# K's minus half on ScalarE by heads, q's softmaxes listed sooner, and three smaller moves in a two-branch linear attention

## The chip, the cores and the metric

The kernel runs on one core of one Trainium2 chip. The metric is the device time of one execution in microseconds (us); lower is better. The core has five engines that run side by side: TensorE (matrix products), VectorE (DVE in the profile), ScalarE (ACT), GpSimd (POOL) and SyncE (SP, which here only issues DMAs). Each has its own queue of instructions and works through it in order.

## The reference

Two branches A and B do the same on the same `x` with their own weights, and a gate mixes them. For one branch, with 2048 rows, 448 columns and 16 heads of 28:

```python
qkv = (x @ wqkv).reshape(B, S, 3, H, Dh).transpose(2, 0, 3, 1, 4)
pq = einsum("bhsd,hdf->bhsf", q, w_phi);  pk = einsum("bhsd,hdf->bhsf", k, w_phi)
phi_q = concatenate([softmax(pq), softmax(-pq)], -1)
phi_k = concatenate([softmax(pk), softmax(-pk)], -1)
kv = einsum("bhsf,bhsd->bhfd", phi_k, v);  z = phi_k.sum(over s)
num = einsum("bhqf,bhfd->bhqd", phi_q, kv)
den = einsum("bhqf,bhf->bhq", phi_q, z) + 1e-6
branch = (num / den) @ wo
...
g = sigmoid((x * gate_w).sum(-1))
out = g * branch_A + (1 - g) * branch_B
```

Everything is float32. So each row has, in each of 32 heads (16 of A, 16 of B), a plus half `softmax(p)` and a minus half `softmax(-p)`, for K and for Q.

## The kernel before, in words

The 2048 rows are 16 tiles of 128. `x` comes transposed, in eight pairs of tiles. TensorE multiplies in a rounded float32 form; to keep precision every operand is split into a high part and a low part (`split_x`, `split_wv`), and a product is 11 matmuls (`XT`: high by high, high by low, low by high).

**Start.** V's weights arrive in two halves (b = 0 is A with the gate's column, b = 1 is B), are split, and `v_first` (L394) computes V of tiles 0 and 1 together, a half at a time. Tile 0 goes to PSUM banks VA and VB, tile 1 borrows the two banks of K (`v_bank`, L387). `load_wp` (L305) brings the feature weights `phi` by four DMAs from ScalarE's queue. `fold` (L321) multiplies them into K's and then Q's projection, so that K and Q come out of TensorE as `p`; it needs `phi` and the loaded weights.

**K phase.** For each tile: `k_proj` (22 matmuls) into one PSUM pair of banks K, copied to `pk` by ScalarE (L439). `k_soft` (L429) then does the two softmaxes over the 28 features of each head: DVE takes the maximum and the minimum (L440, L441); GpSimd subtracts, `pk - max` and `min - pk` (L442, L443); ScalarE takes the exponential of each half in place (L446); DVE sums the heads (L447) and inverts (L448); GpSimd scales (L449). `pk`, `mx` and `sm` have two buffers, the result `e` three. `kv_acc` multiplies the result with V, two tiles at a time. Between them stand V of later tiles, and `q_proj` and `q_front` of Q, which subtract the maximum and send the tile through DRAM (`qd`) to bring four rows' heads together.

**Q's softmaxes** (`q_soft`, "S" in the list): a load from `qd`, exponential, minimum, subtraction, exponential, two sums, a scale, and a DVE transpose (L502) into one of four slots `eT`. One buffer `eq` serves all tiles, so the next tile begins behind that transpose. Tiles 0 to 7 are written to DRAM (`spill`) and fetched later; tiles 8 and 9 stay in slots 0 and 1; tiles 10 to 15 (`JIT = 10`) are done in the last phase.

**Last phase.** After K's last tile: `num` (L530) multiplies two tiles of Q's features with the turned `kv`, DVE transposes the result (L548), `mix` (L553) divides and applies the gate on GpSimd, `o_turn` transposes and splits, `out_mm` does 21 matmuls for each output tile, 42 for a pair.

**Gates.** `gates` (L510) inverts the logits on DVE, sends them through DRAM with five SP DMAs, and ends with a GpSimd operation (L518) that computes 1 - g. It is called for tiles 0 to 11 and, in the last phase, for 12 to 15.

**Order.** `steps()` lists the work; each function records its instructions with `Plan.add`: engine, estimated cost, keys read and written. `Plan.order` (L53) keeps TensorE's instructions in the listed order and lets the others go by a due time, worked backwards from what depends on them. The keys serve only this planning; the waits on the chip follow from the tiles that the instructions truly touch.

Of the kernel before, what the change touches and what calls it, by code (L numbers as in the profile page):

```python
# [9 lines left out]
AF = mybir.ActivationFunctionType  # L10
# [97 lines left out]

def steps():

    yield from (("V01", 0), ("V01", 1), ("FK", 0), ("x1",), ("V", 2), ("FK", 1), ("wq", 0), ("wq", 1), ("V", 3), ("x", 2))
    yield from (("FQ", 0), ("V", 4, 0), ("FQ", 1), ("later",), ("K", 0), ("V", 4, 1), ("K", 1), ("wo_rows",))
    yield from (("Q", 0), ("S", 0, 0), ("K", 2), ("Q", 1), ("S", 1, 1), ("kv", 0, 1), ("K", 3), ("V", 5))
    for p in range(2, 8):
        if p < 7:
            yield "x", p + 1
        yield "K", 2 * p
        yield "Q", 2 * p - 2
        if 2 * p - 2 < JIT:
            yield "S", 2 * p - 2, 0  # L120
        yield "kv", 2 * p - 2, 2 * p - 1
        yield "wo", p - 2
        if p in (3,):
            yield "wo", 6
        if p < 6:
            yield "V", 2 * p + 2
        yield "K", 2 * p + 1
        if p < 7:
            yield "Q", 2 * p - 1
            if 2 * p - 1 < JIT:  # L130
                yield "S", 2 * p - 1, 1
        if p < 6:
            yield "V", 2 * p + 3
        if p == 6:
            yield "gates", 0, 12
# [24 lines left out]
SPILL = list(range(JIT - 2))  # L160


# [1 line left out]
def hedgehog_mix(ctx: ExitStack, tc: tile.TileContext, xd, wv, wkt, wqt, wphi, wo, cmask, cpmask, out):  # L164
# [140 lines left out]
    def load_wp():  # L305
        add("DVE", 0.15, lambda: V.memset(wp, 0.0), [], [("wp", q) for q in range(4)])
        for q in range(4):
            add("ACT", 0.45, lambda q=q: A.dma_start(wp[32 * q:32 * q + DH], wphi[DH * q:DH * q + DH]), [], [("wp", q)], lat=3)
# [66 lines left out]
    def xkeys(t):  # L375
        return [("x", t // 2 % NX, t % 2), ("xl", t // 2 % NX, t % 2)]
# [14 lines left out]
        o, n = ((0, D + 2), (VB, D))[b]  # L391
        return [x[:, :, o:o + n] for x in (wvh, wvl)], n

    def v_first(b):  # L394

        w, n = v_weights(b)
        parts = [([(c, i, c)], [("x", 0, t) for t in range(2)] + [("v" + "hl"[i], c, b)])
                 for c, i in ((0, 0), (1, 0), (0, 1), (2, 0), (1, 1), (3, 0), (2, 1), (3, 1))]
        parts.append(([(4 + c, 0, c) for c in range(3)], xkeys(0) + xkeys(1)))
        for terms, keys in parts:  # L400
            def go(terms=terms):
                for xc, l, c in terms:
                    for t in range(2):
                        n_, k = v_bank(t, b)
                        nc.tensor.matmul(bank[n_][:, k, :n], xs[0][:, xc, t * P:t * P + P], w[l][:, c], start=(xc, l) == (0, 0), stop=xc == 6)
            add("PE", 2 * len(terms) * 0.203, go, keys, [v_bank(t, b)[0] for t in range(2)])
        for t in range(2):
            v_out(t, b)

    def v_proj(t, b):  # L410
# [13 lines left out]

    def k_proj(t, b):
        add("PE", 11 * 0.197, mms(t, feat((wkh, wkl), b), "K", b, FO, FZ),
            xkeys(t) + [("k", h, j, b) for h in "hl" for j in range(4)], ["K"])

    def k_soft(t):  # L429
        def p4():  # L430
            return fm(bank["K"][:, :, FO:FO + D])
        pk, kp = pks[t % 2].rearrange("p b (h f) -> p b h f", f=DH), ("pk", t % 2)
        mx, sm, e, n = mxs[t % 2], sms[t % 2], es[t % NE], t % NE
        ke, km = [("e", n, s) for s in range(2)], [("mx", t % 2, s) for s in range(2)]
        pkh = pk.rearrange("p b h f -> p (b h) f")
# [5 lines left out]
        put("DVE", 2 * D, lambda: V.tensor_reduce(mh[1], pkh, AX.X, OP.min), [kp], [km[1]])  # L441
        put("POOL", 2 * D, tt("POOL", e4[0], pkh, bc[0], OP.subtract), [kp, km[0]], [ke[0]])  # L442
        put("POOL", 2 * D, tt("POOL", e4[1], bc[1], pkh, OP.subtract), [kp, km[1]], [ke[1]])  # L443
        for s in range(2):
            e3 = e[:, s].rearrange("p (h f) -> p h f", f=DH)
            put("ACT", 2 * D, act(e[:, s], e[:, s], AF.Exp), [], [ke[s]])  # L446
            put("DVE", 2 * D, lambda s=s, e3=e3: V.tensor_reduce(sm[:, s], e3, AX.X, OP.add), [ke[s]], [("sm", t % 2, s)])  # L447
# [36 lines left out]
    def q_soft(k, slot):  # L484
# [10 lines left out]
        for s in range(2):  # L495
            e3 = eq[:, s].rearrange("p a c f -> p (a c) f")[:, :, :DH]
            put("DVE", 2 * D, lambda s=s, e3=e3: V.tensor_reduce(qsm[:, s], e3, AX.X, OP.add), [ke[s]], [("qsm", s)])  # L497
# [4 lines left out]
        add("DVE", 2.25, lambda: V.transpose(eTf[slot], eq.rearrange("p s a c f -> p (s a c f)")), ke, [("eT", slot)])  # L502

    def spill(k, slot):
        add("SP", 0.4, dma(ed[k], eTf[slot]), [("eT", slot)], [("ed", k)], lat=3, kb=1048)
# [4 lines left out]
    def gates(lo, hi):  # L510
        gl = glog[:, lo:hi]
        kl = [("gl", t) for t in range(lo, hi)]
        add("DVE", 0.1, lambda: V.tensor_scalar(gl, gl, 1.0, None, op0=OP.add), [], kl)
        add("DVE", 0.2, lambda: V.reciprocal(gl, gl), [], kl)
        add("SP", 0.4, dma(gd[:, lo:hi], gl), kl, [("gd", lo)], lat=2)
        for r in range(4):
            add("SP", 0.4, dma(gate[32 * r:32 * r + 32, 0, :, lo:hi], gd[:, lo:hi].rearrange("(c t) n -> t c n", c=4)), [("gd", lo)], [("ga", lo, r)], lat=2)
        add("POOL", 0.25, lambda: G.tensor_scalar(gate[:, 1, :, lo:hi], gate[:, 0, :, lo:hi], -1.0, 1.0, op0=OP.mult, op1=OP.add),  # L518
            [("ga", lo, r) for r in range(4)], [("gate", t) for t in range(lo, hi)])

    def kv_turn():
        for b in range(2):
# [79 lines left out]
    for b in range(2):  # L602
        for c in range(4):
            load_wv(c, b)
        if b == 0:
            load_wp()
    split_x(0, 0, P, "DVE")
    split_x(0, P, 2 * P, "DVE", "DVE")
    for b in range(2):
        for c in range(4):  # L610
            split_wv(c, b, "DVE" if b == 0 else "POOL")
    load_x(1)
    for b in range(2):
        load_wt(wkt, b)
# [27 lines left out]
    for what, *a in steps():  # L642
# [1 line left out]
            for b in a[1:] or (0, 1):  # L644
                v_proj(a[0], b)
        elif what == "V01":
            v_first(a[0])
        elif what == "K":
            if a[0] == 0:
                plan.hand_over([("x1raw",), *[("wvr", c, b) for c in range(4) for b in range(2)]], [("e", n, s) for n in range(NE) for s in range(2)])  # L650
# [42 lines left out]
            fetch(*a)  # L693
        elif what == "gates":
            gates(*a)
        else:
            {"later": later, "wo_rows": wo_rows, "load_wo": load_wo, "free_k": lambda: plan.hand_over(["K", "VA", "VB"], ["N"], free_k),
             "free_q": lambda: plan.hand_over(["Q"], ["O1", "T1"], free_q), "kv_turn": kv_turn,
# [50 lines left out]
```

## Time and profile before

| what | value |
|---|---|
| median of 3 runs | 352.05 us (349.84 to 352.11) |
| the profiled execution's own time | 351.24 us |
| its span in the profile | 349.5 us |
| granted TensorE clock | 1.00 |
| DVE busy | 277.7 us (79%) |
| ScalarE busy | 143.5 us (41%) |
| GpSimd busy | 245.0 us (70%) |

The profile is that of one execution. The span goes from its first instruction to its last; 1.74 us of the time lie outside it. A busy time is the sum over one engine's instructions with overlaps counted once. "Idle before, releaser" behind a row tells how long the engine had stood still and what ended that. "issue" as a releaser is time in which the engine waited for nothing that the profile shows.

### The profile page before, as it was taken

What the parts mean: (1) busy time and instruction counts of PE and PEld (TensorE: products, weight loads), DVE (VectorE), ACT (ScalarE), POOL (GpSimd) and SP (SyncE); (2) the same over time, 40 slices, a digit from 0 to 9 for tenths busy, and PEclk for the clock granted to TensorE, in tenths of its full rate; (3) what the DMA queues carried; (4) which work ended last, traced back from release to release, by engine and by line L of the source; (5) the groups of instructions that cost most, each with busy time, mean ns of one, the idle gap of its engine ahead of it and who ended that gap; (6) DMA issues with size and microseconds to landing.
All of it is one profiled execution on the core that took longest, in us unless ns stands there. A gap on an engine that the chain in (4) does not pass through costs nothing.

```text
span 349.5 us, 9271 instructions
## 1 busy us (share of the span) xinstructions
PE 333.1 (95%) x3976; PEld 298.5 (85%) x3976; DVE 277.7 (79%) x334; ACT 143.5 (41%) x218; POOL 245.0 (70%) x196
## 2 busy tenths in 40 slices
PE   8898899999999999999999999998989998998995
PEld 7786799899999999999999998997768887787894
DVE  5038679859897954979979899978879999889690
ACT  4556464533562443517336234432042333433231
POOL 1550397999989779869977978894088769767600
PEclk9999999999999999999999999999999999999999
DMA  7998402541656647435464162574974445221102
GB/s 230 260 225 227 149 12 69 171 140 44 220 213 199 223 155 219 191 95 174 128 216 173 56 225 56 146 329 147 312 240 152 158 173 203 88 110 41 45 26 79
DMA packets 29528, 55.21 MB, mean 158 GB/s; under 512 B 4288, under 2 KB 23344, under 8 KB 27184
## 3 DMA queue, kind: packets, MB, share of 16 engines
q1 hardware_dynamic: 28312, 52.68, 46.1%
q10 hardware_dynamic: 1176, 1.95, 2.3%
q8 instruction: 31, 0.51, 0.6%
q14 instruction: 9, 0.07, 0.1%
HBM read 32.00 MB, written 24.22 MB: 161 GB/s over the span
## 4 chain that ended last, share of the span: by engine, by line
DVE 32%; PE 22%; POOL 21%; issue 11%; DMA 8%; ACT 3%; SPq 1%; ACTq 0%; DVEq 0%; POOLq 0%
POOL re L255 10%; PE O L585 7%; POOL rt L255 6%; DVE sm L447 5%; DVE rt L502 4%; PE K L372 4%; DVE ru L255 3%; DVE qsm L497 3%; DVE rv L548 3%; DVE qmx L474 3%; PE Q L372 2%; POOL rv L557 2%; DMA gate<-gd 2%; PE F L326 2%; PE VA L372 2%
## 5 line engine op out<-in xcount | busy, mean ns | idle before, releaser
L585 PE MATMUL O<-rk,rx 128*128 128x448 f32 x336 | 70.4, 368 | 4.4 <-ACT rx L258 4.4
L372 PE MATMUL Q<-rq,rx 128*128 128x432 f32 x352 | 72.1, 360 | 2.0 <-DVE ru L255 2.0
L585 PEld LDWEIGHTS O<-rk,rx 128*128 128x128 f32 x336 | 62.5, 188 | 12.8 <-ACT rx L258 6.4
L372 PE MATMUL K<-rk,rx 128*128 128x432 f32 x352 | 72.2, 360 | 0.0
L372 PEld LDWEIGHTS Q<-rq,rx 128*128 128x128 f32 x352 | 65.9, 188 | 5.9 <-DVE ru L255 2.9
L372 PEld LDWEIGHTS K<-rk,rx 128*128 128x128 f32 x352 | 65.9, 188 | 3.4 <-issue 0.2
L255 POOL TENSOR_TENSOR re<-re,sm 128x896 f32<-128x896 f32 x32 | 53.9, 1707 | 11.9 <-DVE sm L448 8.3
L258 ACT ACTIVATE re<-re 128x896 f32<-128x896 f32 x32 | 30.4, 950 | 44.5 <-POOL re L255 44.5
L447 DVE TENSOR_REDUCE sm<-re 128x32 f32<-128x896 f32 x32 | 33.6, 1072 | 7.4 <-ACT re L258 7.3
L255 POOL TENSOR_TENSOR rt<-qmn,ru 128x896 f32<-128x896 f32 x16 | 28.2, 1765 | 15.1 <-DVE rt L502 11.2
L497 DVE TENSOR_REDUCE qsm<-rt 128x32 f32<-128x896 f32 x32 | 33.6, 1064 | 4.7 <-ACT rt L258 4.7
L372 PE MATMUL VA<-rv,rx 128*128 128x450 f32 x154 | 34.8, 372 | 1.3 <-issue 1.3
L502 DVE STREAM_TRANSPOSE rt<-rt 128x2048 f32<-128x2048 f32 x13 | 29.7, 2286 | 6.8 <-POOL rt L255 6.8
L372 PE MATMUL VB<-rv,rx 128*128 128x448 f32 x154 | 33.5, 365 | 0.0
L258 ACT ACTIVATE rt<-ru 128x896 f32<-128x896 f32 x16 | 15.2, 949 | 44.3 <-issue 21.1
L372 PEld LDWEIGHTS VA<-rv,rx 128*128 128x128 f32 x154 | 28.4, 189 | 4.7 <-issue 2.1
L372 PEld LDWEIGHTS VB<-rv,rx 128*128 128x128 f32 x154 | 29.0, 188 | 2.3
L255 POOL TENSOR_TENSOR re<-pk,mx 128x896 f32<-128x896 f32 x16 | 28.0, 1749 | 3.6 <-DVE mx L440 3.6
L255 POOL TENSOR_TENSOR rt<-rt,qsm 128x896 f32<-128x896 f32 x16 | 27.3, 1705 | 1.1
L255 POOL TENSOR_TENSOR re<-mx,pk 128x896 f32<-128x896 f32 x16 | 27.3, 1707 | 0.0
L557 POOL TENSOR_TENSOR rv<-rv,rd 128x896 f32<-128x896 f32 x14 | 23.8, 1702 | 1.1
L440 DVE TENSOR_REDUCE mx<-pk 128x32 f32<-128x896 f32 x16 | 17.0, 1060 | 7.0 <-ACT pk L258 7.0
(92 smaller groups left out, 461.9 us busy)
## 6 DMA issues: line engine op xcount, KB each, us to landing
ed<-rt SPq DMA_DIRECT2D x8, 1024.0 KB
qd<-ru SPq DMA_DIRECT2D x64, 112.0 KB
ru<-qd SPq DMA_DIRECT2D x16, 448.0 KB
re<-ed SPq DMA_DIRECT2D x5, 1024.0 KB
xraw<-in_xt SPq DMA_DIRECT2D x7, 512.0 KB
out<-re SPq DMA_DIRECT2D x16, 224.0 KB
wod<-wst SPq DMA_DIRECT2D x14, 224.0 KB
rk<-wod SPq DMA_DIRECT2D x2, 1568.0 KB
```

The lines of the kernel that those rows point to most:

```text
L255: return lambda: ENG[eng].tensor_tensor(val(o), val(a), val(b), op)
L258: return lambda: A.activation(val(o), val(i), f, **k)
L326: nc.tensor.matmul(bank["F"][32 * o:32 * o + 32, q, g * P:(g + 1) * P], wpd[32 * q:32 * q + DH, b, g], wt[b][32 * q:32 * q + DH, g].rearra ...
L372: nc.tensor.matmul(bank[name][:, k, lo:hi], x[:, xc, o:o + P], w[l][:, c], start=i == 0, stop=i == len(XT) - 1)
L440: put("DVE", 2 * D, lambda: V.tensor_reduce(mh[0], pkh, AX.X, OP.max), [kp], [km[0]])
L447: put("DVE", 2 * D, lambda s=s, e3=e3: V.tensor_reduce(sm[:, s], e3, AX.X, OP.add), [ke[s]], [("sm", t % 2, s)])
L474: put("DVE", 2 * D, lambda: V.tensor_reduce(mx, p4(), AX.X, OP.max), ["Q"], [km])
L497: put("DVE", 2 * D, lambda s=s, e3=e3: V.tensor_reduce(qsm[:, s], e3, AX.X, OP.add), [ke[s]], [("qsm", s)])
L502: add("DVE", 2.25, lambda: V.transpose(eTf[slot], eq.rearrange("p s a c f -> p (s a c f)")), ke, [("eT", slot)])
L548: add("DVE", 0.07 + 1.08 * nt, lambda: V.transpose(ctr().rearrange("p (r n) -> p r n", r=4), bank["N"][:, :, :2 * nt * P]), ["N"], [("ctr" ...
L557: put(eng, 2 * D, lambda: ENG[eng].tensor_tensor(mid["o", n % 3].rearrange("p (c a f) -> p a c f", c=4, a=8), ctv()[:, :, i, :, :DH], rd[: ...
L585: nc.tensor.matmul(bank[pb][:, 0, :D], a, w, start=i == 0, stop=i == len(terms) - 1)
```

## The change

Five things are changed. (1) K's minus half: instead of a GpSimd subtraction, one ScalarE exponential over 896 columns and a DVE sum, ScalarE runs one exponential of 28 columns for each of the 32 heads, with the head's minimum as its bias, scale -1, and the head's sum as a second output; the planner sees four blocks of eight heads, at 0.09 us a head. (2) A new key `("S", k)`: K's tile t counts, for the planner, as dependent on Q's softmax of tile t - 6 (`SOON`) and earlier ones. (3) The GpSimd operation that ends `gates` becomes a step of its own, `gates_b`; for tiles 12 to 15 it is listed after the second `mix` and made to follow the buffer `("o", 2)`. (4) `phi` is loaded by GpSimd's queue instead of ScalarE's, and listed after the first half of V's weights is split. (5) V's second half is computed for tile 0 first and then for tile 1; beside that, the low parts of V's second half are made by DVE instead of GpSimd.

```diff
-    yield from (("V01", 0), ("V01", 1), ("FK", 0), ("x1",), ...
+    yield from (("V01", 0, 0, 1), ("V01", 1, 0), ("V01", 1, 1), ("FK", 0), ("x1",), ...
...
             yield "gates", 0, 12
+            yield "gates_b", 0, 12
...
+        if p == 1:
+            yield "gates_b", 12, NT, [("o", 2)]
...
-JIT = 10
+JIT, SOON = 10, 6
...
+    def by_head(o, i, sums, least, r, w):
+        for h in range(0, 2 * H, 8):
+            def go(h=h):
+                for k in range(h, h + 8):
+                    A.activation(o[:, k], i[:, k], AF.Exp, bias=least[:, k:k + 1], scale=-1.0, accum_out=sums[:, k:k + 1])
+            add("ACT", 8 * 0.09, go, r, w)
...
     def load_wp():
-            add("ACT", 0.45, lambda q=q: A.dma_start(wp[32 * q:32 * q + DH], wphi[DH * q:DH * q + DH]), [], [("wp", q)], lat=3)
+            add("POOL", 1.0, lambda q=q: G.dma_start(wp[32 * q:32 * q + DH], wphi[DH * q:DH * q + DH]), [], [("wp", q)], lat=3)
...
-    def v_first(b):
+    def v_first(b, ts):
...
-                    for t in range(2):
+                    for t in ts:
...
     def k_proj(t, b):
-            xkeys(t) + [("k", h, j, b) for h in "hl" for j in range(4)], ["K"])
+            xkeys(t) + [("k", h, j, b) for h in "hl" for j in range(4)] + [("S", k) for k in range(t - SOON + 1)], ["K"])
...
     def k_soft(t):
-        put("POOL", 2 * D, tt("POOL", e4[1], bc[1], pkh, OP.subtract), [kp, km[1]], [ke[1]])
         for s in range(2):
             e3 = e[:, s].rearrange("p (h f) -> p h f", f=DH)
-            put("ACT", 2 * D, act(e[:, s], e[:, s], AF.Exp), [], [ke[s]])
-            put("DVE", 2 * D, lambda s=s, e3=e3: V.tensor_reduce(sm[:, s], e3, AX.X, OP.add), [ke[s]], [("sm", t % 2, s)])
+            if s:
+                by_head(e3, pkh, sm[:, s], mh[s], [kp, km[s]], [ke[s], ("sm", t % 2, s)])
+            else:
+                put("ACT", 2 * D, act(e[:, s], e[:, s], AF.Exp), [], [ke[s]])
+                put("DVE", 2 * D, lambda s=s, e3=e3: V.tensor_reduce(sm[:, s], e3, AX.X, OP.add), [ke[s]], [("sm", t % 2, s)])
...
     def q_soft(k, slot):
-        add("DVE", 2.25, lambda: V.transpose(eTf[slot], ...), ke, [("eT", slot)])
+        add("DVE", 2.25, lambda: V.transpose(eTf[slot], ...), ke, [("eT", slot), ("S", k)])
...
+    def gates_b(lo, hi, after=()):
         add("POOL", 0.25, lambda: G.tensor_scalar(gate[:, 1, :, lo:hi], ...),
-            [("ga", lo, r) for r in range(4)], [("gate", t) for t in range(lo, hi)])
+            [("ga", lo, r) for r in range(4)] + list(after), [("gate", t) for t in range(lo, hi)])
...
     for b in range(2):
         for c in range(4):
             load_wv(c, b)
-        if b == 0:
-            load_wp()
...
-            split_wv(c, b, "DVE" if b == 0 else "POOL")
+            split_wv(c, b, "DVE")
+        if b == 0:
+            load_wp()
```

More of the change, by code (lines that the diff above doesn't have):

```diff
@@ L109, in steps @@
 def steps():
-    yield from (("V01", 0), ("V01", 1), ("FK", 0), ("x1",), ("V", 2), ("FK", 1), ("wq", 0), ("wq", 1), ("V", 3), ("x", 2))
+    yield from (("V01", 0, 0, 1), ("V01", 1, 0), ("V01", 1, 1), ("FK", 0), ("x1",), ("V", 2), ("FK", 1), ("wq", 0), ("wq", 1), ("V", 3), ("x", 2))
     yield from (("FQ", 0), ("V", 4, 0), ("FQ", 1), ("later",), ("K", 0), ("V", 4, 1), ("K", 1), ("wo_rows",))
@@ L392, in v_weights @@
         return [x[:, :, o:o + n] for x in (wvh, wvl)], n
-    def v_first(b):
+    def v_first(b, ts):
         w, n = v_weights(b)
-        parts = [([(c, i, c)], [("x", 0, t) for t in range(2)] + [("v" + "hl"[i], c, b)])
+        parts = [([(c, i, c)], [("x", 0, t) for t in ts] + [("v" + "hl"[i], c, b)])
                  for c, i in ((0, 0), (1, 0), (0, 1), (2, 0), (1, 1), (3, 0), (2, 1), (3, 1))]
-        parts.append(([(4 + c, 0, c) for c in range(3)], xkeys(0) + xkeys(1)))
+        parts.append(([(4 + c, 0, c) for c in range(3)], [k for t in ts for k in xkeys(t)]))
         for terms, keys in parts:
@@ L402, in go @@
                 for xc, l, c in terms:
-                    for t in range(2):
+                    for t in ts:
                         n_, k = v_bank(t, b)
                         nc.tensor.matmul(bank[n_][:, k, :n], xs[0][:, xc, t * P:t * P + P], w[l][:, c], start=(xc, l) == (0, 0), stop=xc == 6)
-            add("PE", 2 * len(terms) * 0.203, go, keys, [v_bank(t, b)[0] for t in range(2)])
-        for t in range(2):
+            add("PE", len(ts) * len(terms) * 0.203, go, keys, [v_bank(t, b)[0] for t in ts])
+        for t in ts:
             v_out(t, b)
@@ L501, in q_soft @@
                 put("POOL", 2 * D, tt("POOL", e3, e3, qsm[:, 1, :, None].to_broadcast([P, 2 * H, DH]), OP.mult), [("qsm", 1)], [ke[1]])
-        add("DVE", 2.25, lambda: V.transpose(eTf[slot], eq.rearrange("p s a c f -> p (s a c f)")), ke, [("eT", slot)])
+        add("DVE", 2.25, lambda: V.transpose(eTf[slot], eq.rearrange("p s a c f -> p (s a c f)")), ke, [("eT", slot), ("S", k)])
     def spill(k, slot):
@@ L646, in hedgehog_mix @@
         elif what == "V01":
-            v_first(a[0])
+            v_first(a[0], a[1:])
         elif what == "K":
@@ L695, in hedgehog_mix @@
             gates(*a)
+        elif what == "gates_b":
+            gates_b(*a)
         else:
```

## The prediction

> **What bounds the kernel now.** I read the page first, for the shares of the engines:
>
> ```profile
> span 349.5 us, 9271 instructions
> ...
> PE 333.1 (95%) x3976; PEld 298.5 (85%) x3976; DVE 277.7 (79%) x334; ACT 143.5 (41%) x218; POOL 245.0 (70%) x196
> ```
>
> TensorE is busy for all but 349.5 - 333.1 = 16.4 us; ScalarE is the emptiest engine. So I asked next what TensorE waits for, over the whole span:
>
> ```profile
> PE O L585 <- ACT rx L258: 4.4, 4, 1.6
> PE Q L372 <- DVE ru L255: 2.0, 2, 1.7
> PE F L326 <- issue: 1.4, 1, 1.4
> PE K L405 <- ACT glog L258: 1.4, 1, 1.4
> PE VA L372 <- issue: 1.3, 1, 1.3
> PE VB L594 <- DVE zero L599: 1.1, 1, 1.1
> PE VA L405 <- ACT rv L258: 0.7, 1, 0.7
> PE T L459 <- POOL re L255: 0.4, 2, 0.2
> ```
>
> These are 12.7 us in eight groups; the other 3.7 are the tail after its last matmul. The large ones lie apart, O and Q late (rows below), F, VA and K L405 at the start. Between them the view by windows shows the K phase (columns: length, then busy us of PE, PEld, DVE, ACT, POOL, each with its instructions):
>
> ```profile
> 47.00:232.00 185.00, 184.26 (x1755) 172.19 (x1754) 155.62 (x186) 80.52 (x112) 161.59 (x112) 1.00 0.48 158
> ```
>
> TensorE stands still for 0.7 of 185 us. What the change frees there on DVE (155.6 busy) and GpSimd (161.6) shortens nothing by itself. Its worth can only come from what is late after 210 us, and its cost from ScalarE, if that can no longer keep up. So the stage to read is ScalarE from the first minus half that can begin (tile 0's minimum is there at 48.97 + 1.07 = 50.0 us) to the end of the last one (231.57 + 0.95 = 232.5):
>
> ```profile
> 48.97 1.07 DVE L441 TENSOR_REDUCE mx<-pk 128x32 f32<-128x896 f32 x1
> ...
> 231.57 0.95 ACT L258 ACTIVATE re<-re 128x896 f32<-128x896 f32 x1 [0.28 <-POOL re L255]
> ```
>
> The window between these, and its first 25 us, with ACT alone:
>
> ```profile
> 50.00:232.50 182.50, 79.89 (x111) 1.00 0.49 161
> 50.00:75.00 25.00, 12.04 (x15) 1.00 0.42 122
> ```
>
> **Part 1: the minus half by heads.** It removes all of the third row here and half of the first two (busy us, mean ns of one); the fourth is there for its size:
>
> ```profile
> L447 DVE TENSOR_REDUCE sm<-re 128x32 f32<-128x896 f32 x32 | 33.6, 1072 | 7.4 <-ACT re L258 7.3
> ...
> L258 ACT ACTIVATE re<-re 128x896 f32<-128x896 f32 x32 | 30.4, 950 | 44.5 <-POOL re L255 44.5
> ...
> L255 POOL TENSOR_TENSOR re<-mx,pk 128x896 f32<-128x896 f32 x16 | 27.3, 1707 | 0.0
> ...
> L576 ACT ACTIVATE rx<-rv 128x384 fp32r<-128x384 f32 x8 | 4.1, 516 | 0.0
> ```
>
> Gone are 16 GpSimd subtractions (27.3 us), half of the 32 sums on DVE (16.8 us) and half of the 32 exponentials (15.2 us of ScalarE). In their place come 16 x 32 = 512 exponentials of 28 columns, each with its sum. The trace has none with a column as bias or with a sum, so I bound a head by ScalarE's nearest rows, start to start:
>
> ```profile
> 102.56 0.94 ACT L258 ACTIVATE rt<-ru 128x896 f32<-128x896 f32 x1
> 103.40 0.93 ACT L258 ACTIVATE re<-re 128x896 f32<-128x896 f32 x1
> 104.24 0.53 ACT L258 ACTIVATE vs<-VA 128x448 f32<-128x448 f32 x1
> 104.67 0.16 ACT L258 ACTIVATE glog<-VA 128x1 f32<-128x1 f32 x1
> 104.72 0.55 ACT L258 ACTIVATE vs<-VB 128x448 f32<-128x448 f32 x1
> ```
>
> From 102.56 to 103.40 an exponential of 896 columns holds the engine 0.84 us. Its duration is 0.95, that of the 384-column copy above 0.516, so a column costs (0.950 - 0.516) / 512 = 0.00085 us, 896 of them 0.76, and the fixed share in a row of instructions is 0.84 - 0.76 = 0.08. Alone, with nothing overlapping, the fixed share is 0.950 - 0.76 = 0.19. One column out of PSUM (glog) holds the engine from 104.67 to 104.72, 0.05, and takes 0.16 alone. So a head costs no less than 0.05 (one such step, bias and sum free) and no more than 0.19 + 0.024 for the exponential plus 0.16 for a sum that is read out by itself, none of it overlapped: 0.376. In between I build it of rows: 0.08 + 28 x 0.00085 = 0.104 for the exponential; the bias is another operand to fetch and the sum another result to store, and for 28 columns such fixed shares are nearly everything, so I take 0.08 for each: 0.264. It is nearest to the rows in sequence, since the heads follow each other without a wait.
>
> In the window, 79.89 - 15.2 = 64.7 us of other ScalarE work stay: copies of K and V out of PSUM, the plus halves, Q's exponentials. That leaves 182.5 - 64.7 = 117.8 us, or 0.230 for a head. At 0.264 the heads take 512 x 0.264 = 135.2; the sum is 199.9, and the last K tile is ready 17.4 us later. This cannot be caught up: `kv` needs every tile, and `num` needs `kv`. The lag comes early: in the window from 50 to 75 us, 12.04 - 3 x 0.95 = 9.2 us of other work stand beside four tiles' heads, 4 x 32 x 0.264 = 33.8, so ScalarE is 18 us behind after 25; the rest then just fills its window. The planner, with 0.09 a head, does not see this. Behind the heads in ScalarE's queue stand the copy of K (TensorE's next K tile waits for its bank), the copies of V, and the exponentials of S.
>
> The Trainium skill ("ScalarE: Activation LUTs", section "What ACT_TABLE_LOAD costs") states about 280 ns + 0.833 ns a column for an ACTIVATE with a column as bias, and an overlap of about 93 ns between neighbours; that is, as an estimate, 0.21 us a head before any sum. By it 512 x 0.21 + 64.7 = 172.2 us would just fit the window; no row here has such a bias, and without these two sentences the sum stands.
>
> **Parts 4 and 5: the start.**
>
> ```profile
> 1.44 1.86 ACTq L308 DMA_DIRECT2D wp<-in_wphi  x4
> 3.33 1.28 ACT L258 ACT_TABLE_LOAD   x1 [3.33 <-issue]
> ...
> 11.36 4.11 POOL L255 TENSOR_TENSOR rv<-re,rv 128x448 fp32r<-128x448 f32 x4 [9.81 <-ACT rv L258]
> ...
> 13.56 0.47 PE L405 MATMUL K<-rv,rx 128*128 128x448 f32 x1 [1.38 <-ACT glog L258]
> ...
> 18.42 1.60 PEld L326 LDWEIGHTS F<-rt,wpd 28*32 28x32 f32 x124 [0.25 <-DMA rt<-in_wkt]
> ...
> 20.41 2.32 DVE L330 STREAM_TRANSPOSE rt<-F 128x2048 f32<-128x2048 f32 x1 [10.55 <-PE F L326]
> ```
>
> The four issues leave ScalarE's queue (1.86 us) and the table load can begin some 1.9 us sooner; V's weights then still come when the DMAs bring them. GpSimd's first larger work is the low parts at 11.36, which now are DVE's, so four issues there, at 0.46 (ScalarE's) or at several times that, are covered: `phi` is first used by the fold at about 18. The low parts on DVE are cheap (four of at most GpSimd's 4.11 us together): it stands still for 10.55 us before 20.41. Computing tile 0 first takes away the 1.38 us wait for K's bank, as VB is free. But the fold that follows waited for its weights until 18.42, so TensorE comes to that wait 1.4 us sooner. I take 0 for the start; the ends are -1.4 (those weights come as much sooner) and +1.4 (a shifted order of DMAs brings them later).
>
> **Parts 2 and 3: what is late after 210 us.**
>
> ```profile
> 219.29 4.58 PE L372 MATMUL K<-rk,rx 128*128 128x432 f32 x22
> ...
> 233.95 2.25 DVE L502 STREAM_TRANSPOSE rt<-rt 128x2048 f32<-128x2048 f32 x1
> ...
> 250.27 0.55 DVE L550 RECIPROCAL rd<-rv 128x64 f32<-128x64 f32 x1
> ...
> 253.03 0.21 POOL L518 TENSOR_SCALAR gate<-gate 128x16 f32<-128x16 f32 x1 [8.12 <-DMA gate<-gd]
> ...
> 253.20 0.27 POOL L255 TENSOR_TENSOR rd<-rd,gate 128x32 f32<-128x32 f32 x1
> ...
> 256.70 5.57 PE L585 MATMUL O<-rk,rx 128*128 128x448 f32 x26 [1.61 <-ACT rx L258]
> ```
>
> The transposes of S lie, tile 9's, at 233.95, behind K's tile 15 at 219.29; with the key the planner puts it before. On the chip the key is no wait, and S's DMAs (four stores and a load each, and the spills) only move ahead in SP's queue. With 44 us less on DVE and GpSimd, and both waiting for ScalarE in my forecast, these chains are ahead when K ends. So the 2.0 us of "Q <- DVE ru" go. The gate: 253.03 is when its DMA had landed; the first `mix` operation (253.20) stood behind it though `rd` was there at 250.27 + 0.55 = 250.82. Moved, the operation lets `mix` begin 2.4 us sooner, and the 1.61 us that O waited at 256.70 go. Its new place waits for `("o", 2)`; behind it stand later mixes, and the first to need its result is tile 12's, two pairs on. The rest of "O <- ACT rx", 4.4 - 1.6 = 2.8 us, comes of DVE being nearly full in the last phase (19.6 of 20 us, the third busy time):
>
> ```profile
> 260.00:280.00 20.00, 20.00 (x328) 16.55 (x327) 19.59 (x24) 7.66 (x14) 14.76 (x16) 1.00 0.50 158
> ```
>
> If tile 10's S is ahead, its minimum and two sums leave this stretch, 1.05 + 2 x 1.06 = 3.2 us:
>
> ```profile
> L497 DVE TENSOR_REDUCE qsm<-rt 128x32 f32<-128x896 f32 x32 | 33.6, 1064 | 4.7 <-ACT rt L258 4.7
> ...
> L491 DVE TENSOR_REDUCE qmn<-ru 128x32 f32<-128x896 f32 x16 | 16.8, 1049 | 4.1 <-DMA ru<-qd 3.8 <-POOL rt L255 0.3
> ```
>
> I take half of the 2.8. The sum after 210 us is -(2.0 + 1.6 + 1.4) = -5.0; its ends are -6.4 (all of O and Q) and 0 (the order turns out no better).
>
> **Sum.** Against the profiled execution's 351.24 (its span and 1.74 around it; 0.8 under the median 352.05): 351.2 + 17.4 - 5.0 + 0 = 363.6, so 364.
>
> **The rivals.**
>
> *Heads are cheap (not slower: faster).* If bias and sum ride along free, a head costs 0.05 to 0.12. From 50 to 75 us there is room for (25 - 9.2) / 128 = 0.123; below that ScalarE never lags, and the time is 351.2 - 5.0 = 346.2, at best 351.2 - 6.4 = 344.8. For it: ScalarE is busy 41%, and the glog row shows how small a step can be. Against: it would need two more memory accesses in an instruction that cost nothing, where 0.08 us of every row in sequence is access. The price decides: up to about 0.16 the lag stays under a tile's heads, which the two `pk` buffers absorb. Chance 0.30.
>
> *Only the exponential costs (within 1%).* With its fixed share not overlapped and the sum free, a head costs 0.214; 64.7 + 109.6 = 174.3 us fit into 182.5. But early, 9.2 + 27.4 = 36.6 us stand in 25: 11.6 behind, 6.9 of it (a tile's heads) absorbed, 4.7 lost: 351.2 + 4.7 - 5.0 = 350.9. The rule of the Trainium skill above ("ScalarE: Activation LUTs") is this case. Its price is nearest to a row for the exponential, but leaves the sum at nothing. Chance 0.14.
>
> *Everything costs.* At 0.376, the upper end, 64.7 + 192.5 = 257.2, 74.7 us too many: 421. For it speaks only that no row shows an overlap for such instructions. 0.06 for over 388.
>
> **How the numbers follow.** The forecast has 0.50: ScalarE becomes the bound of the K phase. Its own range goes from 355 (0.247 a head) to 388 (0.311, bias and sum at 0.104 each). The range for 8 in 10 must reach into the cheap case: 344 to 388, with 0.05 below (more than O and Q regained) and 0.06 above. 1% is about what a measurement of this kernel can tell from no change. Faster by over 1%: 0.30. Within 1%: 0.14. Slower: 0.50 + 0.06 = 0.56.
>
> **What would show it.** In the profile after: ScalarE busy near 143.5 - 15.2 + 135 = 263 us, over 95% in the slices from 50 us to K's end, with TensorE's waits naming ScalarE (pk or e) in the first of them; a group of 512 exponentials of 128x28 whose steps are 0.26 us; DVE near 277.7 - 16.8 + at most 4.1 = 265 us and GpSimd near 245.0 - 27.3 - 4.1 = 214; the gate operation without its 8.1 us wait; the wait for glog gone and one for `in_wkt` in its place. The prediction is wrong if the steps are under 0.2 us, or if ScalarE is not the engine that K's tiles wait for.

## The result, and the profile after

The changed kernel took 424.89 us, the median of 4 runs (424.01 to 427.67), beside 352.08 us for the kernel before in the same session: 1.2075 of it, with a 95% interval of 1.2018 to 1.2131. The prediction was 364 us, its range 344 to 388. The profiled execution took 424.01 us. Each ratio here and below is taken over those executions of a kernel that lie within 1.5% of its fastest, so it need not be the ratio of the medians.

The page first, the busy times of the engines:

```profile
span 422.2 us, 10249 instructions
...
PE 355.8 (84%) x3976; PEld 315.4 (75%) x3976; DVE 266.5 (63%) x322; ACT 279.5 (66%) x1226; POOL 217.7 (52%) x180
```

TensorE now stands still for 422.2 - 355.8 = 66.4 us, where it was 16.4. No engine is near its limit over the whole span, ScalarE neither. What TensorE waits for, the largest rows (columns: sum, times, longest, us):

```profile
PE T L472 <- POOL re L258: 32.7, 7, 7.9
PE K L383 <- ACT pk L261: 8.9, 3, 5.0
PE Q L383 <- DVE ru L258: 6.7, 4, 2.8
PE VB L383 <- ACT vs L261: 5.7, 1, 5.7
PE O L600 <- ACT rx L261: 2.2, 3, 1.0
PE K L416 <- ACT glog L261: 2.0, 1, 2.0
```

`kv` (bank T) waits for GpSimd's scaled features, 32.7 us; before, this was 0.4. Where the time lies is read from the last `kv` of the K phase, tiles 14 and 15: the first line is its row before, the second after, each from its own timeline.

```profile
237.11 1.78 PE L459 MATMUL T<-re,vs 128*29 128x56 f32 x128
```

```profile
313.33 1.78 PE L472 MATMUL T<-re,vs 128*29 128x56 f32 x128
```

It starts 76.2 us later. From there to the end of the span it was 349.5 - 237.11 = 112.4 us and is 422.2 - 313.33 = 108.9, so 3.5 us are gained. 76.2 - 3.5 = 72.7 is the difference of the two spans, 422.2 - 349.5. K's first tile begins at 40.95 us before and at 40.37 after, so everything was lost in the K phase: from there to this `kv` it was 196.2 us and is 273.0.

ScalarE in the K phase, a timeline at its first heads, the two groups of the new line, and the view by windows from the first head to the last (columns: length, then busy us of PE, PEld, DVE, ACT, POOL with their instructions, and the granted clock):

```profile
49.88 0.30 ACT L281 ACTIVATE re<-pk,mx 128x28 f32<-128x28 f32 x1
50.09 0.18 ACT L281 ACTIVATION_READ_ACCUMULATOR re<-pk,mx 128x1 f32 x1
50.18 0.30 ACT L281 ACTIVATE re<-pk,mx 128x28 f32<-128x28 f32 x1
```

```profile
L281 ACT ACTIVATE re<-pk,mx 128x28 f32<-128x28 f32 x512 | 154.5, 303 | 27.3 <-DVE mx L452 25.0
L281 ACT ACTIVATION_READ_ACCUMULATOR re<-pk,mx 128x1 f32 x512 | 96.0, 187 | 0.0
```

```profile
49.50:309.80 260.30, 205.56 (x1748) 187.77 (x1747) 145.40 (x174) 217.78 (x1120) 137.45 (x98) 0.89 0.35 118
```

A head with its sum is two instructions, and from one head to the next it is 50.18 - 49.88 = 0.30 us (0.301 over longer rows); 0.21 of it is the exponential, 0.09 the sum's instruction. With 64.7 us of other work this makes 64.7 + 512 x 0.301 = 218.8 us, and ScalarE was busy for 217.8. That is 36 us more than the old window of 182.5 holds. But the window after is 260.3 us long: beside the work there are 260.3 - 217.8 = 42.5 us in which ScalarE stands idle. Both must be explained, 35.3 us of work beyond the old window and 42.5 of idle time; together they are the 77.8 by which the window grew.

The idle time looks like a lap between engines that each wait in order. The largest rows of the waits of ScalarE, DVE and GpSimd (ScalarE's from 49.5 to 310 us, DVE's from 46 to 310, GpSimd's over the span):

```profile
ACT re L281 <- DVE mx L452: 25.0, 10, 3.3
ACT rt L261 <- DVE rt L515: 10.2, 2, 5.8
```

```profile
DVE sm L460 <- ACT re L261: 54.7, 13, 8.7
DVE sm L461 <- ACT re L281: 35.9, 14, 3.7
```

```profile
POOL re L258 <- DVE sm L461: 76.9, 15, 9.3
```

ScalarE waits for the minimum of the next tile (25.0 us; 10.2 more are Q's exponential behind a transpose); DVE stands at the plus half's sum (L460), because that exponential is queued behind another tile's heads on ScalarE, and then at the reciprocal of the minus sums (L461), which needs the last head; GpSimd waits for DVE before it may scale. One round of it, DVE's timeline and ScalarE's:

```profile
196.49 1.03 DVE L504 TENSOR_REDUCE qmn<-ru 128x32 f32<-128x896 f32 x1
197.43 1.07 DVE L451 TENSOR_REDUCE mx<-pk 128x32 f32<-128x896 f32 x1
198.42 1.07 DVE L452 TENSOR_REDUCE mx<-pk 128x32 f32<-128x896 f32 x1
...
205.40 1.08 DVE L460 TENSOR_REDUCE sm<-re 128x32 f32<-128x896 f32 x1 [1.53 <-ACT re L261]
210.22 0.57 DVE L461 RECIPROCAL sm<-sm 128x32 f32<-128x32 f32 x2 [3.73 <-ACT re L281]
```

```profile
195.38 0.91 ACT L261 ACTIVATE pk<-K 128x896 f32<-128x896 f32 x1
199.59 0.32 ACT L281 ACTIVATE re<-pk,mx 128x28 f32<-128x28 f32 x1 [3.30 <-DVE mx L452]
...
204.43 0.94 ACT L261 ACTIVATE re<-re 128x896 f32<-128x896 f32 x1
```

At 196.3 ScalarE has copied K. The tile's heads stand next in its queue, so it stands still for 3.30 us while DVE, which is busy then, does a minimum for Q and K's maximum and minimum, about 1 us each. It is so in ten of the sixteen tiles, 1.7 to 3.3 us each time. In this round it then runs sixteen heads ahead of a plus exponential (204.43), for which DVE waits; after that sixteen more, for which DVE waits again at 210.22.

That is what the traces suggest. The experiments were to tell apart three things: the price of a head (work), the order that the planner made at 0.09 us a head (idle time), and what the other four parts do.

### The profile page after: what moved, and what is told of

Read it like the earlier page. It is cut to its first block, busy times and chain, and to the rows that moved or that the text cites. A ratio compares the mean times of both kernels' runs of the same rounds, so it can differ in the third digit from the quotient of the medians.

```text
span 422.2 us, 10249 instructions
## 1 busy us (share of the span) xinstructions
PE 355.8 (84%) x3976; PEld 315.4 (75%) x3976; DVE 266.5 (63%) x322; ACT 279.5 (66%) x1226; POOL 217.7 (52%) x180
## 4 chain that ended last, share of the span: by engine, by line
ACT 44%; DVE 20%; PE 15%; POOL 8%; DMA 6%; issue 5%; SPq 1%; ACTq 0%; POOLq 0%; DVEq 0%
ACT re L281 35%; PE O L600 6%; DMA qd<-ru 3%; ACT re L261 3%; DVE qsm L510 3%; POOL rt L258 3%; DVE mx L451 3%; DVE rv L563 3%; DVE mx L452 3%; POOL re L258 2%; ACT rt L261 2%; PE VB L383 2%; DMA re<-in_xt 2%; PE VA L383 2%; PE F L337 2%
## 5 line engine op out<-in xcount | busy, mean ns | idle before, releaser
L281 ACT ACTIVATE re<-pk,mx 128x28 f32<-128x28 f32 x512 | 154.5, 303 | 27.3 <-DVE mx L452 25.0
L281 ACT ACTIVATION_READ_ACCUMULATOR re<-pk,mx 128x1 f32 x512 | 96.0, 187 | 0.0
L383 PE MATMUL K<-rk,rx 128*128 128x432 f32 x352 | 79.8, 386 | 8.9 <-ACT pk L261 8.9
L383 PEld LDWEIGHTS K<-rk,rx 128*128 128x128 f32 x352 | 72.1, 207 | 14.3 <-ACT pk L261 10.0
L460 DVE TENSOR_REDUCE sm<-re 128x32 f32<-128x896 f32 x16 | 17.3, 1084 | 54.7 <-ACT re L261 54.7
L472 PE MATMUL T<-re,vs 128*29 128x56 f32 x1024 | 19.5, 242 | 32.7 <-POOL re L258 32.7
L472 PEld LDWEIGHTS T<-re,vs 128*29 128x29 f32 x1024 | 16.9, 127 | 36.1 <-POOL re L258 34.0
L383 PE MATMUL VA<-rv,rx 128*128 128x450 f32 x154 | 39.2, 407 | 3.0 <-issue 1.5
L383 PEld LDWEIGHTS VA<-rv,rx 128*128 128x128 f32 x154 | 32.2, 214 | 7.4 <-issue 1.9
L461 DVE RECIPROCAL sm<-sm 128x32 f32<-128x32 f32 x32 | 9.6, 330 | 36.1 <-ACT re L281 35.9
```

What stands on the lines that cost most here:

```text
L281: A.activation(o[:, k], i[:, k], AF.Exp, bias=least[:, k:k + 1], scale=-1.0, accum_out=sums[:, k:k + 1])
L383: nc.tensor.matmul(bank[name][:, k, lo:hi], x[:, xc, o:o + P], w[l][:, c], start=i == 0, stop=i == len(XT) - 1)
L472: nc.tensor.matmul(kvp()[32 * r:32 * r + DH + 1, b, g], vs[t % NV][:, b, h // 2, h % 2], es[t % NE][:, :, hs:hs + DH], start=(t == 0 and b ...
```

## The experiments

The runs came in three sessions; the median of the kernel before was 352.3, 352.2 and 353.8 us in them. Where there is no interval, a single execution stands for a kernel; the intervals of the kernels with wo's splits, with 0.209 in the plan, on odd tiles and with the heads but without part 2 rest on two. That is enough for differences of 10 us and more.

**The change without the heads.** Parts 2 to 5 alone:

```diff
+        put("POOL", 2 * D, tt("POOL", e4[1], bc[1], pkh, OP.subtract), [kp, km[1]], [ke[1]])
...
-            if s:
-                by_head(e3, pkh, sm[:, s], mh[s], [kp, km[s]], [ke[s], ("sm", t % 2, s)])
-            else:
-                put("ACT", 2 * D, act(e[:, s], e[:, s], AF.Exp), [], [ke[s]])
...
```

> The changed kernel with the minus half put back as it was (GpSimd subtraction, one exponential of 896 columns, DVE sum); the four other parts stay. By the prediction's terms for those parts: 351.2 - 5.0 = 346.2 us, no lower than 344.8, and slower than before only if the other parts cost something themselves. If the heads alone make the loss, all 73 us of it must be gone.

Measured: 353.75 us, 1.0049 of before (1.0014 to 1.0083). So these parts do not gain 5 us, as the 346.2 had it; they lose a little, under 1%. The last phase did gain (352.0 - 243.15 = 108.9 us), but `kv` of tiles 14 and 15 starts at 243.15, 6.0 us late. TensorE's timeline shows why:

```profile
219.12 0.99 PE L470 MATMUL T<-re,vs 128*29 128x56 f32 x64 [2.20 <-POOL re L258]
222.44 1.72 PE L470 MATMUL T<-re,vs 128*29 128x56 f32 x64 [2.32 <-POOL re L258]
224.09 5.83 PE L383 MATMUL K<-rk,rx 128*128 128x432 f32 x22
```

and DVE's and GpSimd's what it waited for:

```profile
213.55 0.93 DVE L459 RECIPROCAL sm<-sm 128x32 f32<-128x32 f32 x4
```

```profile
213.72 0.26 POOL L258 TENSOR_TENSOR qsm<-qsm 128x32 f32<-128x32 f32 x1 [4.04 <-DVE qsm L510]
214.05 1.70 POOL L258 TENSOR_TENSOR rt<-rt,qsm 128x896 f32<-128x896 f32 x1
215.71 6.67 POOL L258 TENSOR_TENSOR re<-re,sm 128x896 f32<-128x896 f32 x4
```

DVE inverts the sums of four halves of K at once, late, behind S's two sums (207.13, 2.07 us) and reciprocal, and on GpSimd S's scaling (`rt<-rt,qsm`) stands before the four scalings of K that have collected. Behind the two waits the 22 matmuls of K take 5.83 us instead of 4.58: the granted clock was lower there (0.91 from 200 to 240 us, 1.00 in the kernel before).

**The heads alone**, in the kernel before:

```diff
-        put("POOL", 2 * D, tt("POOL", e4[1], bc[1], pkh, OP.subtract), [kp, km[1]], [ke[1]])
...
+            if s:
+                by_head(e3, pkh, sm[:, s], mh[s], [kp, km[s]], [ke[s], ("sm", t % 2, s)])
...
```

> The kernel before with the minus half by heads and nothing else of the change. If the heads alone make the loss: 424 us plus the 4 to 5 that the other parts give back, 426 to 432. If Q's softmaxes, listed sooner, stand in ScalarE's queue ahead of the heads and block them (they wait 10.2 us for the transposes in the changed kernel), it is quicker without that key: 405 to 415.

Measured: 437.6 us, above both expectations (426 to 432, 405 to 415); `kv` waits 36.1 us for GpSimd, Q 15.6 for DVE. With the heads the other parts give back 12.7 us, though without them they cost one or two. The second expectation, that S's key makes the loss, does not fit: without it the time is longer.

**The whole change, the planner told the measured price.**

```diff
-            add("ACT", 8 * 0.09, go, r, w)
+            add("ACT", 8 * 0.301, go, r, w)
```

> The changed kernel, with the planner's price of a head at the measured 0.301 us instead of 0.09; the instructions are the same, only their order can change. ScalarE's sum (154 us of heads and 64.7 of other work into 182.5) gives 382; 42 us of the 424 are beyond that. If they come of an order planned on a wrong price: 380 to 392, with ScalarE idle under 12 us between its first and last head (42 now). If they come of the listed order of TensorE, which lets K run only one tile ahead of kv, so that copy, minimum, heads, scaling and kv follow each other: 412 to 426.

Measured: 398.86 us, between the two expectations, with the same work in another order. From the first head to the end of the last, then what ScalarE's wait (46 to 300 us) and DVE's (46 to 310) of the lap have become:

```profile
46.00:266.10 220.10, 192.06 (x1744) 178.26 (x1743) 141.68 (x169) 212.34 (x1113) 130.85 (x92) 0.92 0.36 113
```

```profile
ACT re L281 <- DVE mx L452: 3.2, 5, 2.0
```

```profile
DVE sm L460 <- ACT re L261: 2.8, 6, 0.5
```

ScalarE idles 220.1 - 212.3 = 7.8 us instead of 42.5, and the two waits are 3.2 and 2.8 instead of 25.0 and 54.7. So most of the idle time, 34.7 of 42.5 us, was the order's. (DVE's other wait, L461, fell from 35.9 to 13.8 us, and `kv` still waits 22.9 us for GpSimd.) In the last phase something new is late:

```profile
PE O L600 <- DMA rk<-wod: 15.3, 2, 14.3
```

wo's splits had been pushed behind K by the dearer heads; less this wait the time would be near 384, if the splits cost nothing elsewhere.

**wo's splits sooner.** Two kernels, both with 0.301, in which K's later tiles wait in the plan for wo's splits, from tile 8 or from tile 12 on (the second is shown):

```diff
-            ... + [("S", k) for k in range(t - SOON + 1)], ["K"])
+            ... + [("S", k) for k in range(t - SOON + 1)] + [("wod", i, c) for c in (*range(t - 10), 6) for i in range(2) if t > 11], ["K"])
```

> The changed kernel with the plan told 0.301 us a head (398.9 us, of which 15.3 were the first output product's wait for wo, split too late) and K's tiles after the fourth pair made to wait in the plan for wo's splits, so that these are spread over K's phase. Theory (the bound is ScalarE's sum: 64.7 + 512 x 0.301 = 218.8 us from 50 us on, then the last phase): the 15.3 us wait goes and the time is 380 to 387 us, ScalarE over 95% busy from 50 to 266 us. Rival (the last phase stays behind something else, the fetches of q's stored tiles or the softmaxes pushed after K): 393 to 400 us with another wait in the place of wo's.

> The changed kernel, 0.301 us a head in the plan, wo's splits tied in the plan to K's tiles from the thirteenth on. Tied from the ninth on, the wait for wo went, the last phase took 108.9 us, but the first head began 7 us later (53.0 for 46.0) and ScalarE idled 15.1 us for 7.8 in K's phase, so the time stayed at 398.8. Theory (ScalarE's 216 us of work from the first head on, then a last phase of 109, is the bound): first head near 46, heads done by 266 to 270, 380 to 387 us. Rival (wo's splits cost K's phase what they save after it, wherever they stand): 394 to 400 us.

Measured: 398.78 us (1.1331, 1.1235 to 1.1428) and 396.54 (1.1208, 1.0897 to 1.1519). Both rivals came out by the time, and these runs and the 398.86 lie too close to be told apart. The first rival's reason did not hold: the wait for wo is gone and the last phase took 108.9 us in both (398.8 - 289.88; 392.2 - 283.33). The second rival's did in the main. In the second kernel the first head began at 49.94 us, and

```profile
49.94:278.90 228.96, 193.69 (x1753) 178.98 (x1751) 143.85 (x173) 216.20 (x1120) 138.96 (x99) 0.93 0.42 133
```

so its span is 49.9 + 216.2 of ScalarE's work + 12.8 idle + 4.4 until `kv` + 108.9 = 392.2. Against the kernel of 398.86 us, the first head 3.9 us later and 5.0 us more idle took back part of the gain, and so did the 3.9 us by which this window holds more of ScalarE's work (wo's splits among it). I did not reach the 380 to 387: what wo's splits save after the K phase, they seem to cost before or in it, in the two places tried.

**The heads without their sum output**, at the plan's 0.09; DVE sums as before:

```diff
-                    A.activation(o[:, k], i[:, k], AF.Exp, bias=least[:, k:k + 1], scale=-1.0, accum_out=sums[:, k:k + 1])
+                    A.activation(o[:, k], i[:, k], AF.Exp, bias=least[:, k:k + 1], scale=-1.0)
...
+                put("DVE", 2 * D, lambda s=s, e3=e3: V.tensor_reduce(sm[:, s], e3, AX.X, OP.add), [ke[s]], [("sm", t % 2, s)])
```

> The changed kernel with the heads' exponentials but without their second output; the sums are made by DVE as before. A head should step in 0.209 us instead of 0.301. By ScalarE's sum alone (107 + 64.7 = 172 into 182.5) the time is the 350.9 us of the prediction's second rival. If K's lap (copy, minimum, heads, scaling, kv, next K) bounds, each pair of tiles saves 2 x 3 us of its 35 and the DVE sum gives 1 back: 424 - 7 x 5 = 389, 380 to 395.

Measured: 382.94 us, in the range of the lap (380 to 395) and far from the sum's 350.9; a tile's 32 heads take 6.7 us, 0.209 each:

```profile
49.69 6.78 ACT L281 ACTIVATE re<-pk,mx 128x28 f32<-128x28 f32 x32
56.37 0.91 ACT L261 ACTIVATE pk<-K 128x896 f32<-128x896 f32 x1
```

ScalarE's work, 64.7 + 512 x 0.209 = 171.7 us, would fit the old window, and yet 31 us are lost. **The same with 0.209 in the plan** (`8 * 0.209`):

> The changed kernel with heads without their sum output (VectorE sums, as before), and the plan told 0.209 us a head, the step measured, in place of 0.09. With 0.09 it took 382.9 us and ScalarE idled for long in K's phase. Theory (the plan's order, not the 0.209, cost the 31 us): ScalarE's work of 64.7 + 512 x 0.209 = 171.7 us fits its window of 182.5, so 350 to 358 us with no lap between ScalarE and K's tiles. Rival (the dependence of each K tile on its exponential makes the loop long whatever the order): 370 to 385 us.

Measured: 364.52 us (1.0358, 1.0272 to 1.0444), between the two expectations. The order cost 18.4 of the 31 us. The rest stays: ScalarE is busy 169.9 of the 198.8 us from the first head to the last, and `kv` waits 11.3 us for GpSimd. K's first tile begins at 44.67 us there, 40.95 before, so 3.7 us of the loss lie ahead of the K phase; why, I have not found out.

**Neither sum nor bias**, 0.09 in the plan, DVE sums as before: the kernel leaves out the minimum, and the minus half is the exponential of -K alone.

```diff
-                    A.activation(o[:, k], i[:, k], AF.Exp, bias=least[:, k:k + 1], scale=-1.0, accum_out=sums[:, k:k + 1])
+                    A.activation(o[:, k], i[:, k], AF.Exp, scale=-1.0)
...
```

> The changed kernel with heads that have neither the sum output nor the least value as bias (the minus half is then the exponential of minus K alone; VectorE sums as before). It measures the step of one head: 0.209 us with bias, 0.301 with bias and sum. If the bias by partition has a fixed price of 0.08 as the prediction's sum had it: about 0.13 us. If it costs nothing and a 28-column exponential has one fixed price: 0.20 to 0.21 us. The time itself follows the step: 355 to 370 in the first case, 380 to 386 in the second.

```profile
50.21 3.81 ACT L281 ACTIVATE re<-pk 128x28 f32<-128x28 f32 x32
```

3.81 / 32 = 0.119 us a head: the bias by partition costs 0.209 - 0.119 = 0.090. One execution took 355.38 us, beside 353.79 for the kernel before. Step and time are those of the first case. From K's first tile to `kv` of 14 and 15 it took 244.69 - 42.91 = 201.8 us, the change without the heads 243.15 - 41.23 = 201.9: at this price, with a plan near it, the heads cost nothing, and they gain nothing either.

**Heads on odd tiles alone**, 0.301 in the plan:

```diff
+        if t % 2 == 0:
+            put("POOL", 2 * D, tt("POOL", e4[1], bc[1], pkh, OP.subtract), [kp, km[1]], [ke[1]])
...
-            if s:
+            if s and t % 2:
```

> The changed kernel with minus by heads on odd tiles alone (256 heads, the even tiles as before), 0.301 us a head in the plan. ScalarE's work in K's phase is 64.7 + 256 x 0.301 + 8 x 0.95 = 149 us for a window of 182.5, so by the sum it costs nothing. If the sum is what sets the time once the plan has the price: 350 to 355 us. If the length of a tile's chain counts (9.6 us on ScalarE in place of 1.7 on GpSimd and 0.95 on ScalarE, for every second tile): 358 to 372 us, with kv waiting for scalings.

Measured: 371.94 us (1.0513, 1.0412 to 1.0614). By ScalarE's sum it should cost nothing. In its trace:

```profile
PE T L474 <- POOL re L258: 12.2, 6, 6.0
```

Of the 21.4 us by which the span grew (349.5 to 370.9), 4.2 lie ahead of K's first tile (45.16 for 40.95), again for a reason that I have not found, and the K phase took 261.97 - 45.16 = 216.8 us instead of 196.2. So with the price in the plan and room on ScalarE the chain of a tile still seems to count: 32 x 0.301 = 9.6 us on ScalarE stand where 1.7 us on GpSimd and 0.95 on ScalarE stood, and everything that ScalarE owes to others waits behind them. This agrees with the 364.52 of the heads without sum. That the chain, and not the order, sets it is argued, not shown: I have not separated how much of it a better order could still remove.

**Part 2 undone, with the heads** and **without them**; in both

```diff
-JIT, SOON = 10, 6
+JIT, SOON = 10, 99
```

> The changed kernel with part 2 alone undone: K's tiles do not wait in the plan for q's softmaxes. The heads alone took 437.6 us, the whole change 424.9, so that the other parts gave back 12.7 with the heads, though they cost a little without them (1.005 of before; 0.993 with part 2 undone as well). Theory (part 2 gives it back: it keeps q's softmaxes in the stretch where K's tiles are late and does not leave them to a late end): 435 to 440 us. Rival (part 2 hurts with the heads as without them, the start's parts or the gate operation give it back): 418 to 424 us.

> The changed kernel without minus by heads, and without the rule that K's tiles wait in the plan for q's softmaxes (part 2 undone too). Without the heads it took 353.75 us, and in its trace kv(14,15) started 6.0 us later than before, behind a 4.7 us wait of kv for scalings that came late because S is sooner. Theory (part 2 pushes K's sums and scalings aside): those waits go, kv(14,15) starts at 237 to 239 and the end follows: 346 to 349.5 us. Rival (the delay comes from the start, phi on GpSimd and V01's second half by tile): 352 to 354 us, kv(14,15) still near 243.

Measured with the heads: 438.85 us (1.2404, 1.2009 to 1.2799), within 1.3 us of the heads alone; Q waits 14.1 us for DVE where the whole change has 6.7. So with the heads it is part 2 that gives back the 12.7 us, as the theory had it. Without the heads: 351.53 us, 0.9933 of before (0.989 to 0.9976), between the two expectations. Its interval lies apart from that with part 2 (1.0014 to 1.0083); but its twelve executions spread from 347.91 to 355.56 us, and by the medians of all executions it is 351.53 against 352.16, 0.998, where the kernel with part 2 has 1.004. So without the heads part 2 costs something between 0.6% and 1.2%. The wait of `kv` is gone (0.4 us for 4.7), and from K's first tile to `kv` of 14 and 15 it took 197.7 us, with part 2 201.9, before 196.2. In the profiled execution, at 354.28 us a long one, this `kv` still starts at 242.61, since K's first tile came 4.0 us later there (44.95 for 40.95); there V's second half of tile 1 waited 3.2 us for K's bank.

**The gate operation alone**, in the kernel before: `gates_b` as in the change, nothing else.

> Before with the gate's operation listed later and nothing else (part 3 alone). The last phase (from the start of kv(14,15) to the end) was 112.4 us before and 108.9 in both runs with this part. Theory (the 3.5 us of the last phase are the gate operation's place on GpSimd): 348 to 349.5 us with a last phase near 109 us. Rival (they come from S being done sooner): 351.5 to 352.5 us, last phase near 112.

Measured: 350.54 us, 0.9953 of before (0.9915 to 0.9992). The last phase took 348.6 - 238.60 = 110.0 us, 2.4 less than before, and O waits 2.2 us instead of 4.4. That is between theory and rival: 2.4 of the 3.5 us are the gate operation's place. The other 1.1 need part 2: without it the change without heads has 352.5 - 242.61 = 109.9 us, and Q's wait in the last phase is 1.7 us, with it 0.7. This kernel and the change without heads and without part 2 are the two with a ratio under 1; their intervals overlap, and by them the gain is between 0.1% and 1.1%, by the medians 0.5% and 0.2%.

## Why the prediction was wrong, point by point

**What bounds the kernel, and where a change can count.** Right: the cost came from ScalarE in the K phase and nowhere else, and what the change freed on DVE (277.7 to 266.5 us) and GpSimd (245.0 to 217.7) shortened nothing. Both busy times were forecast within 4 us.

**The price of a head.** The form was right, the size low. Three fixed shares of 0.08 and 0.024 for the columns made 0.264; measured are 0.119 for exponential and columns (a fixed share of 0.095), 0.090 for the bias and 0.092 for the sum, together 0.301. The share read from the sequence of 896-column exponentials was too small by 0.01 to 0.015 each, 0.037 a head, 512 x 0.037 = 18.9 us in all. The price of a column had been read too high: from the step of 0.84 for 896 columns to that of 0.119 for 28 it is 0.00083 us, not 0.00085, which leaves 0.096 for the fixed share. With the right price the step "lag = work beyond the window" gives 36.3 instead of 17.4, and the sum 382.5: still in the range. The Trainium skill ("ScalarE: Activation LUTs", section "What ACT_TABLE_LOAD costs") gives the first two shares: with 186 ns for constants, 93 more for each operand by partition and 93 of overlap, 28 columns make, as an estimate, 0.116 and 0.21 us, and the runs have 0.119 and 0.209.

**That the lag is ScalarE's sum alone.** This is the step that failed. The text says that the planner "does not see this", and then counts as if ScalarE, once late, would never stand still. The term for ScalarE's idle time was put at nothing without a reason; it was 42.5 us. The planner set the queues of all engines by 0.09 us a head, so minima, sums and scalings stood in an order that fits heads of 2.9 us a tile, not 9.6. With the price put right the idle time fell to 7.8, two of the lap's three largest waits nearly vanished, and `kv` of tiles 14 and 15 came at 272.81, 40.5 us sooner; 15.3 of these were given back to the wait for wo, so that 25.1 us of span were gained (422.2 to 397.1). The profiles divide the 76.8 us by which the K phase grew (196.2 to 273.0) like this: 36.3 are the sum's, with the measured price; 32.3 went with the right price in the plan, where wo's splits stay in the K phase (283.33 - 42.64 = 240.7); the cause of the other 8.2 stays open.

**ScalarE over 95% busy from 50 us on, TensorE's waits naming it first.** Not so: 217.8 of 260.3 is 84%, and the first wait names GpSimd. ScalarE is behind that at two removes, through the reciprocal of the minus sums on DVE. The total of 263 us of ScalarE was 279.5, nearly all of it by the price.

**Parts 4 and 5.** 0 was forecast. In the change without heads K's first tile begins at 41.23 us instead of 40.95. But the mechanism was not as described: the wait for `glog` did not go; it grew from 1.38 to 1.96 us in the whole change and 2.37 in that without heads, because tile 1 still uses K's banks and is only later in the list. With that the fold comes no sooner to its weights.

**Parts 2 and 3.** -5.0 was forecast; the last phase gave -3.5. The gate operation was right: with this part alone the first mix operation comes 13.8 us behind `kv` of 14 and 15 instead of 16.1, and the last phase is 2.4 us shorter. Of the remaining 2.8 us of O's wait half was to go; 2.2 stay. Of Q's 2.0, 1.3 went in the change without heads. Missed was the price of part 2: S's operations go ahead of K's in the queues of DVE and GpSimd. I looked only for what they free after 210 us, and not for who stands behind them before that: `kv`, 4.7 us, and a lower clock after it (the change without heads). With the heads the same step gave back 12.7 us, so its sign depends on the rest.

**The rivals.** *Heads are cheap* and *only the exponential costs* fell with the 0.301. But they would have been wrong for their time, too: the second said 350.9 at 0.214, and at 0.209 it took 382.9, with the price in the plan 364.5. Only at 0.119 a head (355.4 us) does the time come near it. *Everything costs* had the time, 421, by luck: its reason was 0.376 a head with no overlap, and the heads took 0.301. It was the upper end of a range whose other ends were all prices; no rival had the order of the queues in it, though the sentence on the planner named it.

## What to carry to other kernels

An instruction that a planner places has two prices: what it takes on its engine, and what a wrong figure in the plan does to the order of all others. When a change adds many instructions at an assumed price, work out the price first, and if it is off, count idle time in a lap between engines beside the sum of the work; here 42.5 us of idle time stood beside 35.3 us of work beyond the window. An engine with room on average is no cover for a step that makes one tile's chain several times as long: look at what else is in its queue, and who waits for that. (That is argued from the heads on odd tiles, where a better order was not tried.)

## What the runs showed of the hardware

ScalarE's sum output is an instruction of its own, with a duration of 187 ns and 92 ns in a row of heads. The granted clock was lower where TensorE had waited: 0.89 in the K phase of the changed kernel, 1.00 in its last phase. In the change without the heads, right after the two waits of 2.2 and 2.3 us (the clock is the third number from the end):

```profile
224.00:226.00 2.00, 2.00 (x13) 1.81 (x6) 0.94 (x1) 1.21 (x2) 2.00 (x3) 0.50 0.00 0
226.00:230.00 4.00, 4.00 (x20) 3.77 (x20) 3.74 (x6) 1.69 (x3) 4.00 (x3) 0.90 0.34 104
```

TensorE was busy throughout and had half its clock from 224 to 226 us; ahead of the waits, from 205 to 216.9 us, it was 1.00. So there a wait cost more than its own length: K's 22 matmuls behind it took 5.83 us, in the kernel before 4.58. The Trainium skill ("TensorE: Matmul & The Clock Gate", Part 1) has the same two rates, half the clock after an idle window and the full one after a busy window of some 3.4 us. Here neither of the two waits alone was as long as that, with 1 us of `kv` between them.
